# 64-bit weights decoded by one pass on ScalarE and two on VectorE, and the order of all engines' work set anew

## The chip, the cores and the metric

The kernel runs on one core of a Trainium2 chip. The metric is the device time of one execution in microseconds (us); the median of several runs counts. The core's engines work side by side, each through its own list of instructions in order: TensorE (PE in the profile, its weight loads PEld), VectorE (DVE), ScalarE (ACT), GpSimd (POOL) and SyncE (SP), which here only issues transfers. The 16 DMA engines carry those transfers.

## What is computed

Three layers, one after the other, on 2304 rows: attention with a window of 128 positions (8 heads of 64), a layer with a softmax-weighted activation and a layer norm (512 to 1024 to 512), and a gated layer (512 to 2048 to 512). Cut to what matters:

```python
scores = scale * np.matmul(q, k.transpose(0, 1, 3, 2))      # (4, 8, 576, 576), masked to a window of 128
attn = softmax(scores + bias)
x = np.matmul(attn, v).transpose(0, 2, 1, 3).reshape(2304, 512)
h = x @ w_in                                                # 512 x 1024
solu = h * softmax(h)
ln = (solu - mean) / sqrt(var + 1e-6) * g_ln
x = ln @ w_out                                              # 1024 x 512
h = x @ w2_in                                               # 512 x 2048
out = (h * sigmoid(h)) @ w2_out                             # 2048 x 512
```

The four weight matrices are float64: a weight lies in memory as 8 bytes, two 32-bit words, low and high. All else is float32.

## The kernel before, in words

The rows are cut into 18 blocks of 128 (index i), and two blocks make a chunk (index c, 0 to 8). For a block: the scores of four pairs of heads on TensorE (`a_qk`, L615), mask and maximum on VectorE (L640), the exponential on ScalarE (L645), a split of the result into a high and a low float16 part (`a_parts`), a transpose by DMA (L672) or on TensorE (`turned_parts`, L520 to L523), the product with v (L692), the division (L705), and the same split and transpose for the next product. Then `m1_in` (L734) multiplies with w_in, `layer_norm` follows (L748 to L776), and for a chunk `m1_out` (L826) multiplies with w_out, `m2_in` (L863) with w2_in in eight steps j, and `m2_out` (L890) with w2_out. Every product is made of three float16 products: high by high, high by low, low by high.

The weights stay in SBUF as such pairs, 48 slots of 128x512: w_in in slots 0 to 7, w_out in 8 to 15, w2_in in 16 to 31, w2_out in 32 to 47. `load_weight` brings two slots at a time into a buffer `stage` (two of these, loads at L436, 512 KB each). `decode` turns the 64-bit pattern into a float32 by integer operations in three passes over 128x1024 on VectorE: L414 shifts the high word by 3 into the PSUM tile `bits`, L416 puts the top two bits back, L418 adds the top bits of the low word and writes slot pair `W`. There are 24 decodes. Of each matrix the sum of squares is taken (L444 to L462: squares on ScalarE or GpSimd, a column sum on TensorE, a reduction on VectorE), `norm_scale` makes a power of two of it (the last row is L400; `sw2in` is that of w2_in), and only then does `split_weight` scale and split the slots: scaling at L490 (ScalarE) or L487 (GpSimd), the high part at L335 (ScalarE), the low part at L340 (GpSimd), or, where the letter of the slot in `E_W` is V, the two steps L480 (ScalarE) and L482 (VectorE). So no `m2_in` can start before all eight decodes of w2_in (decodes 9 to 16) and its scale are done, and no `m2_out` before those of w2_out (17 to 24). Each of `xT`, `lnT`, `y16`, `e1` and the PSUM tile `mm1` has one buffer, so ahead of the first `m2_in` only four blocks of `m1_in` and one chunk of `m1_out` can run.

The order of the instructions is made before the launch by a list scheduler in the kernel (`Sched.solve`). Every operation has a priority, set by its kind and block in `at`, and costs in ns for each engine that may take it; the scheduler fills the engines by priority and writes out each engine's list. Where an operation may run on two engines, letters in tables (`ENG`, `E_W`) or the scheduler's estimate choose. SyncE's list is such a list too: a transfer whose source or buffer isn't ready holds up all behind it.

## Time and profile before

| | |
|---|---|
| median of 3 runs | 751.68 us (748.95 to 751.75) |
| span of the profiled execution | 748.5 us, first to last instruction; the runs above are 0.45 to 3.25 us longer |
| busy: PE, PEld, DVE, ACT, POOL | 685.3, 458.8, 450.9, 400.5, 111.7 us |
| moved by DMA | 79.22 MB, mean 106 GB/s |

Busy time is the time in which an engine executes instructions; an average over the span mixes the stage in which weights arrive with the later one in which TensorE works without pause. PEclk in a stretch is the granted clock of TensorE as a share of full speed, 1.00 being 2.4 GHz and 0.50 being 1.2 GHz. The DMA share is the busy time of the core's 16 DMA engines in a stretch, over its length; in short stretches it can come out above 1.

### The profile page before, as it was taken

Reading aid. Unit: us, or ns where it says so; the run is one execution under the profiler, and the core shown is the slowest. Engines: PE = TensorE matmul, PEld = TensorE weight load, DVE = VectorE, ACT = ScalarE, POOL = GpSimd, SP = SyncE. Lnnn points to the kernel's source line nnn. Section 1 sums busy time; section 2 is a strip of 40 time slices with the busy share of each in tenths; the row PEclk is TensorE's granted clock in tenths of the full one; section 3 lists DMA queues with packets and bytes.
Section 4 is the critical chain, followed back from the end, with each engine's and each line's share of the span. In section 5 each row is a group of like instructions: output and inputs, shape, how many; then the busy total and the mean of one; then the engine's idle time right before and its main releaser. Section 6 shows DMA issues by size and latency. Waiting matters only on the chain.

```text
span 748.5 us, 13814 instructions
## 1 busy us (share of the span) xinstructions
PE 685.3 (92%) x5382; PEld 458.8 (61%) x5382; DVE 450.9 (60%) x1167; ACT 400.5 (54%) x850; POOL 111.7 (15%) x96
## 2 busy tenths in 40 slices
PE   2475777989999999999999999999999999999998
PEld 1233344776766558765666677757667767857853
DVE  3899899989868884887716655641552362222220
ACT  5597758998598864666714464431432352232231
POOL 2075321443276110100000100000100000000000
PEclk9996757899999999999999999999999999999999
DMA  9899996477864652847612235121210300200000
GB/s 244 281 301 235 221 258 207 140 156 173 167 122 107 146 125 51 151 105 152 154 29 43 62 81 85 29 57 23 42 36 15 57 29 4 54 29 1 2 28 29
DMA packets 139809, 79.22 MB, mean 106 GB/s; under 512 B 121696, under 2 KB 122336, under 8 KB 139744
## 3 DMA queue, kind: packets, MB, share of 16 engines
q1 hardware_dynamic: 139744, 78.34, 44.6%
q8 instruction: 42, 0.69, 0.4%
q14 instruction: 23, 0.19, 0.1%
HBM read 44.24 MB, written 4.72 MB: 65 GB/s over the span
## 4 chain that ended last, share of the span: by engine, by line
PE 80%; DVE 8%; DMA 5%; ACT 3%; issue 2%; POOL 1%; SPq 0%; DVEq 0%; ACTq 0%
PE mm L890 25%; PE mm L863 23%; PE mm L826 13%; PE mm L734 11%; PE sa L615 4%; PE sa L692 3%; DVE bits L416 1%; DVE W L418 1%; DVE e L640 1%; DMA stage<-in_moe_w_out_dram 1%; DVE bits L414 1%; DMA stage<-in_moe_w_in_dram 1%; DMA k<-in_kn_dram 1%; DMA lnT<-ln 1%; DMA aT<-a 1%
## 5 line engine op out<-in xcount | busy, mean ns | idle before, releaser
L863 PE MATMUL mm<-y,W 128*128 128x256 f16 x1728 | 210.4, 273 | 1.8 <-DVE t L873 1.8
L890 PE MATMUL mm<-W,g 128*128 128x512 f16 x864 | 207.5, 379 | 0.0
L863 PEld LDWEIGHTS <-W 128*128 128x128 f16 x1728 | 165.9, 98 | 39.3 <-issue 2.6
L890 PEld LDWEIGHTS <-g 128*128 128x128 f16 x864 | 82.5, 98 | 74.9 <-issue 0.2
L826 PE MATMUL mm<-lnT,W 128*128 128x256 f16 x864 | 110.0, 277 | 2.3 <-DVE aT L523 1.5
L734 PE MATMUL mm<-W,xT 128*128 128x512 f16 x432 | 103.2, 391 | 2.4 <-DVE W L482 0.9
L826 PEld LDWEIGHTS <-W 128*128 128x128 f16 x864 | 84.5, 99 | 22.8 <-DVE aT L523 1.8
L645 ACT ACTIVATE e<-e,mx 128x256 f32<-128x256 f32 (+1 forms) x144 | 70.1, 488 | 43.1 <-DVE mx L640 38.4
L876 DVE SCALAR_TENSOR_TENSOR g<-t,g 128x512 f16<-128x512 f32 x72 | 50.9, 708 | 59.9 <-ACT g L875 59.7
L875 ACT ACTIVATE g<-t 128x512 f16<-128x512 f32 x72 | 45.1, 627 | 75.8 <-PE mm L890 63.5
L872 ACT ACTIVATE t<-mm,cs 128x512 f32<-128x512 f32 x72 | 48.7, 679 | 60.1 <-PE mm L863 59.9
L873 DVE SCALAR_TENSOR_TENSOR t<-t,mm 128x512 f32<-128x512 f32 x72 | 48.9, 683 | 51.3 <-ACT t L872 50.9
L615 PE MATMUL sa<-k,q 64*128 64x128 f32 x544 | 58.4, 335 | 20.9 <-DVE mx L640 14.9
L734 PEld LDWEIGHTS <-xT 128*128 128x128 f16 x432 | 42.4, 100 | 52.8 <-issue 8.8
L615 PEld LDWEIGHTS sa<-k,q 64*128 64x128 f32 x544 | 42.7, 214 | 46.6 <-DVE mx L640 25.9
L640 DVE CUSTOM_DVE_ANT_0 e<-sa,table 128x256 f32<-128x256 f32 (+1 forms) x144 | 55.1, 401 | 26.5 <-PE sa L692 13.8
L692 PEld LDWEIGHTS <-aT 128*128 128x128 f16 x816 | 33.8, 102 | 20.7 <-DMA aT<-a 9.4
L692 PE MATMUL sa<-vs,aT 128*128 128x64 f16 x816 | 37.9, 200 | 8.5 <-DMA aT<-a 4.8
L335 ACT ACTIVATE a<-e 128x512 f16<-128x512 f32 (+1 forms) x68 | 40.3, 597 | 8.7 <-DMA aT<-a 7.8
L834 DVE SCALAR_TENSOR_TENSOR y<-mm,cs,y 128x512 f16<-128x512 f32 x18 | 13.5, 750 | 49.2 <-ACT y L831 49.2
L340 POOL TENSOR_TENSOR a<-e,a 128x512 f16<-128x512 f32 (+1 forms) x28 | 31.1, 1114 | 75.3 <-ACT a L335 74.7
L340 POOL TENSOR_TENSOR W<-W 128x512 f16<-128x512 f32 x31 | 37.7, 1230 | 25.8 <-ACT W L335 25.8
(133 smaller groups left out, 685.5 us busy)
## 6 DMA issues: line engine op xcount, KB each, us to landing
stage<-in_moe_w_in_dram SPq DMA_DIRECT2D x24, 512.0 KB, 6.0
stage<-in_moe_w_out_dram SPq DMA_DIRECT2D x24, 512.0 KB, 4.9
vraw<-in_vt_dram SPq DMA_DIRECT2D x34, 256.0 KB, 4.0
...
aT<-a SPq DMA_TRANSPOSE x68, 3.5
lnT<-ln SPq DMA_TRANSPOSE x34, 3.2
```

The costliest lines, as they stand in the source:

```text
L340: "G": ("G", cg(n), lambda: G.tensor_tensor(dst(), a(), b(), op), True)}
L615: T.matmul(SA[:, j, sl * P:(sl + 1) * P], q[rows, p, :], k[rows, p, :], start=True, stop=sl not in blank)
L640: v(n + 20, lambda j=j: V.tensor_tensor_reduce(e[:, j, lo:lo + n], SA[:, j, lo:lo + n], table[:, 2 * p + j, o:o + n], -0.125, 3.0e38, ALU. ...
L645: act(n, lambda j=j: A.activation(e[:, j, lo:lo + n], e[:, j, lo:lo + n], AF.Exp, bias=mx[:, j:j + 1], scale=-1.0, accum_out=rs[:, 2 * p + ...
L692: T.matmul(heads()[:, h // 4, h % 4, :], t[:, (2 * ha + j) * nh + c, :], vb[sl][:, h, hv, :], start=(n == 0), stop=(n == 3 * nh - 1))
L734: T.matmul(pt[:, half * 512:(half + 1) * 512], x[:, hx, k, :], W16(2 * k + half, hw), start=(k == 0 and hx + hw == 0), stop=(k == KD - 1 a ...
L826: T.matmul(pt[:, ct % 2], W16(8 + k, hw)[:, ct * P:(ct + 1) * P], l[:, hx * KF1 + k, :], start=(k == 0 and hw + hx == 0), stop=(k == KF1 - ...
L863: T.matmul(pt[:, mm], W16(16 + 4 * k + m // 4, hw)[:, (m % 4) * P:(m % 4 + 1) * P], y[:, hx, k, :], start=(k == 0 and hw + hx == 0), stop= ...
L872: act(512, lambda: A.activation(t.tile, flat(pt.tile), AF.Tanh, scale=cs[:, 0:1]), [pt, (cs, 0)], [t], extra=1)
L873: v(512, lambda: V.scalar_tensor_tensor(out=t.tile, in0=t.tile, scalar=1.0, in1=flat(pt.tile), op0=ALU.add, op1=ALU.mult), [t, pt], [t])
L876: v(512, lambda: V.scalar_tensor_tensor(out=flat(g[:, 1]), in0=t.tile, scalar=2.0 ** -16, in1=flat(g[:, 0]), op0=ALU.mult, op1=ALU.subtrac ...
L890: T.matmul(pt.tile, g[:, hg, mm, b * P:(b + 1) * P], W16(32 + m, hw), start=(m == 0 and hg + hw == 0), stop=(m == KF2 - 1 and hg == 1))
```

## The change

For 22 of the 24 decodes (`DECODE` has an A) the high word is shifted and its top bits set by one instruction on ScalarE: Prelu, which multiplies the positive and the negative values by different constants, read from `stage` with a step of two words and written to `bits`. VectorE multiplies the low word in place by 2^-29 and caps it at 7, and a second pass joins the two into `W`. Decodes 1 and 12 keep the three passes.

Three more things change. The scaling on GpSimd (`tensor_scalar`) has a second operand, a multiplication by 1.0. For scaling, high part, low part and squares a table `PICK` now names the engine of each instruction, VectorE among them also where it was not a choice before. And the priorities are set anew: each kind has a slope of its own over the blocks and 308 single offsets (`LATER`).

```diff
     def at(self, kind, i, p=0):
-        self.prio = PITCH * i + RANK[kind] + 0.01 * p
+        self.prio = RANK[kind] + SLOPE.get(kind, PITCH) * i + 0.01 * p + LATER.get((kind, i), 0.0)
...
+    def scaled(pick, n, dst, src, by, r, w, pool=False):
+
+        alts = [("A", ca(n, 1), lambda: A.activation(dst(), src(), AF.Identity, scale=by()), False),
+                ("V", cv(n, True), lambda: V.tensor_scalar(dst(), src(), by(), None, ALU.mult), True)]
+        if pool:
+            alts.append(("G", cg1(n), lambda: G.tensor_scalar(dst(), src(), by(), 1.0, ALU.mult, ALU.mult), True))
+        s.op(alts, r, w, pick=pick)
...
+        if DECODE[at // 2] == "A":
+            both = [(st, 0), (st, 1)]
+
+            act(1024, lambda: A.activation(flat(t.tile.bitcast(F32)), flat(st.tile.bitcast(F32)[:, :, :, 1]), AF.Prelu,
+                                           scale=2.0 ** 16, alpha=-2.0 ** 32), both, [t])
+            v(1024, lambda: V.tensor_scalar(flat(st[:, :, :, 0]), flat(st[:, :, :, 0]), 2.0 ** -29, 7.0, ALU.mult,
+                                            ALU.min), both, [(st, "low")], fast=True)
+            v(1050, lambda: V.scalar_tensor_tensor(out=out(), in0=t.tile, scalar=3, in1=st[:, :, :, 0],
+                                                   op0=ALU.logical_shift_left, op1=ALU.bitwise_or),
+              [(st, "low"), t], w)
+            return
...
-                if E_W[b] == "H":
-                    pool_(512, lambda: G.tensor_scalar(W[:, a, :], W[:, a, :], scl(), None, ALU.mult),
-                          [(W, a), src], [(W, a)])
-                else:
-                    act(512, lambda: A.activation(W[:, a, :], W[:, a, :], AF.Identity, scale=scl()),
-                        [(W, a), src], [(W, a)], extra=1)
-                copy("A", 512, lambda: W16(b, 0), lambda: W[:, a, :], [(W, a)], [(W, b)])
-                combine("G", 512, ALU.subtract, lambda: W16(b, 1), lambda: W[:, a, :], lambda: W16(b, 0),
+                scaled(("wc", b), 512, lambda: W[:, a, :], lambda: W[:, a, :], scl, [(W, a), src], [(W, a)], True)
+                copy(("wh", b), 512, lambda: W16(b, 0), lambda: W[:, a, :], [(W, a)], [(W, b)])
+                combine(("wl", b), 512, ALU.subtract, lambda: W16(b, 1), lambda: W[:, a, :], lambda: W16(b, 0),
                         [(W, a), (W, b)], [(W, b)])
...
+DECODE = "BAAAAAAAAAABAAAAAAAAAAAA"
...
-V_AT = [0, 1, 5, 9]
+V_AT = [0, 1, 5, 10]
```

What the new priorities make of the lists is seen in the lists themselves. In the new kernel L431 and L433 are the two VectorE passes of a decode, L429 is the Prelu, L341 and L352 are a high and a low part on VectorE, L346 is a scaling there, L412 the last row of `norm_scale`, L459 the weight load, and L690, L571 and L590 are the transfers that were L672, L553 and L572.

**VectorE, a decode of w2_in.** Before, rows around decode 14; `lnst` are the statistics of a layer norm, `xm` the attention's result:

```order
L748 TENSOR_REDUCE lnst<-mm_824 128x1
L414 TENSOR_SCALAR bits<-stage 128x1024
L749 TENSOR_SCALAR lnst<-lnst,sig_151 128x1
L416 SCALAR_TENSOR_TENSOR bits<-stage,bits 128x1024
L418 SCALAR_TENSOR_TENSOR W<-stage,bits 128x2x512
L752 TENSOR_SCALAR lnst<-lnst,sig_151 128x1
L705 TENSOR_TENSOR xm<-sa,rinv 128x512
```

The change, rows around decode 13:

```order
L431 TENSOR_SCALAR stage<-stage 128x1024
L767 TENSOR_SCALAR lnst<-lnst,sig_151 128x1
L486 TENSOR_REDUCE accw2in<-mm 128x1
L341 CAST a_909<-e 128x512
L433 SCALAR_TENSOR_TENSOR W<-bits,stage 128x2x512
L770 TENSOR_SCALAR lnst<-lnst,sig_151 128x1
L474 TENSOR_TENSOR sq<-W 128x512
L723 TENSOR_TENSOR xm<-sa,rinv 128x512
L772 RECIPROCAL lnst<-lnst 128x1
```

Three passes of a decode have become two, and passes that ScalarE or GpSimd had (a high part `a`, a square `sq`) stand between them.

**SyncE, the last loads of w2_in.** Before, with the loads of decodes 15 and 16 (`x4`) and then those of w2_out; `vraw` are rows of v, `aT` and `xT` transposes:

```order
L553 DMA vraw<-in_vt_dram 128x512
L672 DMA_TRANSPOSE aT<-a_959 128x8x128
L672 DMA_TRANSPOSE aT<-a_969 128x8x128
L436 DMA stage<-in_moe_w_in_dram 128x1024 x4
L553 DMA vraw<-in_vt_dram 128x512 x3
L553 DMA vraw<-in_vt_dram 128x256
L436 DMA stage<-in_moe_w_out_dram 128x1024 x2
L720 DMA_TRANSPOSE xT<-x_781 128x8x128
```

The change, with the loads of decode 16 (`x2`) and then those of decodes 17 to 19:

```order
L607 DMA k<-in_kn_dram 128x512
L608 DMA q<-in_qn_dram 128x512
L459 DMA stage<-in_moe_w_in_dram 128x1024 x2
L571 DMA vraw<-in_vt_dram 128x512
L690 DMA_TRANSPOSE aT<-a_1021 128x8x128
L459 DMA stage<-in_moe_w_out_dram 128x1024 x2
L690 DMA_TRANSPOSE aT<-a_1038 128x8x128
L459 DMA stage<-in_moe_w_out_dram 128x1024 x4
```

Ahead of the loads of decode 16 the new list has one load of v and two transposes `aT` less; behind them the loads of decodes 17 to 19 stand closer.

**VectorE, from the last sum of w2_in to its scale.** Before, the row `accw2in` is the last of the four sums, and the row of `sw2in` comes 14 rows behind this piece:

```order
L748 TENSOR_REDUCE lnst<-mm_1134 128x1
L462 TENSOR_REDUCE accw2in<-mm 128x1
L702 TENSOR_SCALAR rinv<-rsum 128x8
L749 TENSOR_SCALAR lnst<-lnst,sig_151 128x1
L703 RECIPROCAL rinv<-rinv 128x8
L392 TENSOR_REDUCE nrmb<-accw2in 128x1
L414 TENSOR_SCALAR bits<-stage 128x1024
L523 TENSOR_TENSOR lnT<-mm,lnT 128x4x128
L640 ISA e,mx<-sa,table 128x256
L640 ISA mx 128x1
```

The change, where the row of `sw2in` comes 9 rows behind the piece:

```order
L431 TENSOR_SCALAR stage<-stage 128x1024
L486 TENSOR_REDUCE accw2in<-mm 128x1
L433 SCALAR_TENSOR_TENSOR W<-bits,stage 128x1024
L723 TENSOR_TENSOR xm<-sa,rinv 128x512
L831 TENSOR_SCALAR shra<-mm 128x1
L404 TENSOR_REDUCE nrmb<-accw2in 128x1
L598 SCALAR_TENSOR_TENSOR vs<-vraw,sv_87,vs 128x8x64
L832 SCALAR_TENSOR_TENSOR shra<-mm,shra 128x1
L405 TENSOR_SCALAR nrmb<-nrmb 128x1
L770 TENSOR_SCALAR lnst<-lnst,sig_151 128x1
```

Before, of decode 17 only the first pass stands ahead of `sw2in`; now both of its passes do, so its loads are waited for as well.

## Rows read from the trace of the kernel before

**Rows 1.** Six stretches: busy us (and instructions) of each engine.

```profile
core 0: us, PE busy (x) PEld busy (x) DVE busy (x) ACT busy (x) POOL busy (x), PEclk, DMA share, GB/s
0.00:127.75 127.75, 75.78 (x519) 42.38 (x519) 107.89 (x259) 89.42 (x218) 40.93 (x45) 0.82 0.94 256
127.75:149.56 21.81, 20.32 (x140) 14.40 (x136) 20.25 (x50) 19.62 (x37) 11.39 (x10) 0.81 0.41 119
149.56:219.55 69.99, 64.90 (x665) 50.44 (x662) 58.38 (x152) 56.17 (x133) 29.35 (x23) 1.00 0.76 157
219.55:748.50 528.95, 524.34 (x4070) 351.61 (x4067) 264.40 (x711) 235.35 (x465) 30.07 (x20) 1.00 0.29 62
0.00:112.00 112.00, 63.53 (x416) 34.84 (x417) 93.33 (x211) 77.29 (x187) 40.93 (x45) 0.82 0.96 257
112.00:127.75 15.75, 12.25 (x104) 7.53 (x102) 14.56 (x51) 12.13 (x31) 0.00 (x0) 0.82 0.82 248
```

**Rows 2.** The three decode passes, by groups: busy us, mean ns | idle before.

```profile
L414 DVE TENSOR_SCALAR bits<-stage 128x1024 uint32<-128x1024 uint32 x24 | 29.3, 1220 | 4.0 <-DMA stage<-in_moe_w_in_dram 3.4 <-DMA stage<-in_moe_w_out_dram 0.6
L416 DVE SCALAR_TENSOR_TENSOR bits<-stage,bits 128x1024 uint32<-128x1024 uint32 x24 | 29.3, 1222 | 0.1
L418 DVE SCALAR_TENSOR_TENSOR W<-stage,bits 128x1024 uint32<-128x1024 uint32 x24 | 29.1, 1213 | 0.1
```

**Rows 3.** Waits of VectorE for weight loads: us, times, longest.

```profile
DVE bits L414 <- DMA stage<-in_moe_w_in_dram: 3.4, 3, 2.7
```

**Rows 4.** Issues of transfers, from the page; KB each, us to landing.

```profile
stage<-in_moe_w_in_dram SPq DMA_DIRECT2D x24, 512.0 KB, 6.0
```

**Rows 5.** Timeline of VectorE and SyncE; start us, us.

```profile
127.75 0.14 DVE L400 TENSOR_SCALAR sw2in<-nrmd 128x1 f32<-128x1 f32 x1
102.28 4.06 SPq L436 DMA_DIRECT2D stage<-in_moe_w_in_dram  x4
```

**Rows 6.** Timeline of TensorE, where its dense work begins; start us, us.

```profile
130.46 13.28 PE L826 MATMUL mm<-lnT,W 128*128 128x256 f16 x96 [1.49 <-DVE aT L523]
143.58 5.34 PE L734 MATMUL mm<-W,xT 128*128 128x512 f16 x24
149.56 1.48 PE L863 MATMUL mm<-y,W 128*128 128x256 f16 x12
219.55 2.75 PE L890 MATMUL mm<-W,g 128*128 128x512 f16 x12
```

**Rows 7.** Groups by shape that price the added passes: busy us, mean ns.

```profile
L774 DVE TENSOR_SCALAR e<-e,lnst 128x1024 f32<-128x1024 f32 x6 | 4.9, 811 | 0.1
L334 DVE CAST x<-xm 128x512 f16<-128x512 f32 x7 | 3.0, 424 | 6.5 <-DMA xT<-x 6.5
L339 DVE TENSOR_TENSOR a<-e,a 128x512 f16<-128x512 f32 x36 | 25.2, 702 | 8.6 <-ACT a L335 8.5
L640 DVE CUSTOM_DVE_ANT_0 e<-sa,table 128x256 f32<-128x256 f32 x128 | 51.0, 416 | 23.9 <-PE sa L692 12.8 <-PE sa L615 9.0 <-PE sa L621 0.8
L523 DVE TENSOR_TENSOR aT<-mm,aT 128x512 f16<-128x512 f32 x4 | 2.7, 683 | 0.2 <-ACT aT L522 0.2
L759 ACT ACTIVATE mm<-e,lnst 128x1024 f32<-128x1024 f32 x18 | 19.9, 1108 | 5.9 <-DVE lnst L758 5.9
L335 ACT ACTIVATE W<-W 128x512 f16<-128x512 f32 x31 | 18.8, 618 | 0.5 <-POOL W L340 0.5
L449 ACT ACTIVATE sq<-W 128x512 bf16<-128x512 f32 x22 | 12.8, 620 | 7.2 <-DVE W L418 4.1 <-DVE nrmb L389 2.9
L487 POOL TENSOR_SCALAR W<-W,sw2out 128x512 f32<-128x512 f32 x6 | 10.6, 1781 | 0.5 <-DVE sw2out L400 0.5
L340 POOL TENSOR_TENSOR W<-W 128x512 f16<-128x512 f32 x31 | 37.7, 1230 | 25.8 <-ACT W L335 25.8
```

**Rows 8.** Timelines of GpSimd and VectorE at one moment; start us, us.

```profile
53.04 1.16 POOL L340 TENSOR_TENSOR W<-W 128x512 f16<-128x512 f32 x1 [1.29 <-ACT W L335]
53.15 1.07 DVE L537 COPY sig<-sig 64x3 f32<-64x3 f32 x1
```

More of the change, by code (lines that the diff above doesn't have):

```diff
@@ L85, in before, with op @@
         return self.pred.get(o, ())
-    def op(self, alts, r=(), w=(), dma=0):
+    def op(self, alts, r=(), w=(), dma=0, pick=None):
+        if pick is not None:
+            name, j = pick
+            alts = [x for x in alts if x[0] == PICK[name][j]] or alts
         o = Op(alts, self.prio, len(self.ops), dma)
@@ L318, in cg, with cg1 @@
         return 215 + 1.98 * n
+    def cg1(n):
+        return 215 + 1.05 * n
     def v(n, fn, r=(), w=(), fast=False, port=False):
@@ L401, in norm_scale, with decode @@
         return big, scl
-    def decode(st, slots):
+    def decode(st, slots, at):
         t = Buf(ps_early, [P, 2, 512], U32, "bits", 1)
@@ L974 @@
 PITCH = 3.3
-RANK = {"table": -104.3, "vnorm": -66.9, "vload": 632.4, "vsplit": 82.3, "load": -243.6, "qk": -57.4,
-        "max": -161.5, "exp": 217.8, "parts": -218.7, "aturn": -111.4, "av": 179.9, "evac": -188.6,
-        "xturn": -57.5, "in": -119.2, "max1": 91.3, "norm": -233.0, "lparts": -421.0, "out": -334.0,
-        "share": -317.7, "y": -192.5, "in2": 186.3, "gate": -449.4, "out2": 257.1, "store": -337.1}
-WAT = {0: (65.8, 0.0, 85.1, 0.0), 8: (-155.1, 0.0, -336.6, 0.0), 16: (49.3, 0.0, 5.2, 0.0),
-       32: (144.1, 0.0, -16.4, 0.0)}
@@ L987, in WEIGHT @@
-def WEIGHT(slot0, at, split=False):
-    a, b, c, d = WAT[slot0]
-    return c + d * at if split else a + b * at
+RANK = {"aturn": 3681.5, "av": 497.5, "evac": -1913.9, "exp": 3035.5, "gate": -1087.6, "in": -116.5, "in2": 365.8,
+        "load": -2917.0, "lparts": -2005.2, "max": -131.3, "max1": 221.3, "norm": -5561.5, "out": -734.9,
+        "out2": 653.6, "parts": -1369.3, "qk": 489.8, "s0": 76.7, "s16": 404.9, "s32": -1212.4, "s8": 2638.4,
+        "share": -580.0, "store": 2676.3, "table": -3238.9, "vload": 7.5, "vnorm": 206.7, "vsplit": 377.6,
+        "w0": 1305.9, "w16": 17.6, "w32": 1146.2, "w8": 16.7, "xturn": -509.3, "y": 209.5}
@@ new lines @@
+SLOPE = {"aturn": 35.85, "av": -12.14, "evac": 25.91, "exp": 11.88, "gate": -14.56, "in": 18.98, "in2": -2.05,
+         "load": 13.07, "lparts": 3.11, "max": -4.74, "max1": 19.24, "norm": -7.64, "out": 20.97, "out2": 18.8,
+         "parts": -5.19, "qk": 19.89, "s0": 18.25, "s16": 6.74, "s32": 2.73, "s8": 8.69, "share": 12.97,
+         "store": 1.79, "table": 26.88, "vload": 9.62, "vnorm": 19.65, "vsplit": -0.07, "w0": -2.23, "w16": -5.62,
+         "w32": -0.22, "w8": -3.53, "xturn": 24.33, "y": -19.05}
```

96 lines of the change are left out of this document (69 added, 27 removed), and 25 rows, old and new, of the table LATER.

## The prediction

> **What bounds the kernel now.** I read the stretches first [rows 1]. From 219.55 us on TensorE is busy for 524.34 of 528.95 us at full clock; from 149.56 to 219.55 us it loses 5.1 of 69.99 us. The time that could be saved lies ahead of that: up to 127.75 us TensorE works 75.78 us, while VectorE is busy for 107.89 us (84%; 93.33 of the first 112 us, 83%, and 14.56 of the next 15.75). The page's other full resource is loading: up to 112 us the DMA share is 0.96 at 257 GB/s, 28.8 MB. So two things are nearly full at once, VectorE and the DMA engines, and that is the crux here.
>
> Next the timelines, for what ends this stretch. `sw2in`, the scale of w2_in, is ready at 127.75 us [rows 5]; the dense work of TensorE begins with `m1_out` of the first chunk (L826) at 130.46 us, goes on with `m1_in`, and the first `m2_in` (L863) stands at 149.56, the first `m2_out` (L890) at 219.55 us [rows 6]. Since no `m2_in` can run before all of w2_in is decoded and scaled, and the buffers allow only one chunk ahead of it, an earlier `sw2in` moves the whole rest. Thirdly the decodes: 24 times three passes of 1.22 us, 87.7 us of VectorE [rows 2]. It waited for loads of w_in and w2_in (one name in the rows) in only three places, 3.4 us together [rows 3], so it kept up with loading and no more.
>
> **The change, part by part.** All sums are against the profiled execution, 748.5 us; the runs shown are 0.45 to 3.25 us above it, so its span and the median differ by 3.2 us, and I add one or two.
>
> *VectorE up to the scale of w2_in.* Of the three passes the old list has 17, 16 and 16 ahead of `sw2in`: 49 x 1.22 = 59.7 us. The new one has two decodes of the old kind (6 passes, 7.3 us) and 15 of each new pass. The second new pass is like L418, 1.213 us: 18.2 us. The first, a multiplication with two operands from SBUF to SBUF, isn't in the trace; the nearest row is L774, of the same shape and form, at 811 ns, and the bound above is L414, which reads `stage` with the same step of two words at 1220 ns [rows 2, 7]. I take 0.81, since both its sides are in SBUF where L414 writes PSUM: 12.2 us (18.3 at the bound). Saved: 59.7 - 37.7 = 22.0 us (15.9).
>
> The new lists hand work to VectorE in return, ahead of the same row: 13 more casts and scalings of 512 columns at 424 ns (5.5 us), four more subtractions and five squares at about 0.7 (6.1 us, the lone small rest included) [rows 7]. Against that six mask passes (L640, 416 ns and a short reading behind each) and three turned parts (L523, 683 ns) now stand behind it, with some small ones: -5.8 us. Net: 22.0 - 11.6 + 5.8 = 16.2 us less (10.1 with the first pass at the bound). By VectorE alone `sw2in` would come at 127.75 - 16.2 = 111.5 us.
>
> *ScalarE and GpSimd.* A Prelu of 128x1024 isn't in the trace. The nearest row is L759, 1024 elements of float32 with PSUM on one side, 1108 ns; bounds are twice the 618 of a 512-column pass (1.24 us) and, if each sign took a pass of its own, 2.2 us [rows 7]. I take 1.1: 22 x 1.1 = 24 us. In exchange it loses some 52 us of high parts, scalings and squares over the whole span, so it gets freer by 28 us; at 2.2 it would still gain 4. The Prelu stands ahead of both VectorE passes' end and adds its 1.1 us once, to the last decode. The second operand on GpSimd costs nothing or saves some of 1781 ns per scaling; the engine worked 40.93 of the first 127.75 us, which covers it [rows 1].
>
> *Loading caps this.* Before, the loads of decodes 15 and 16 were issued from 102.28 us on, and with 6.0 us from issue to landing the last was there at about 112 us, VectorE waiting little [rows 4, 5]. The new SyncE list has one load of v and two transposes less ahead of decode 16 (about 0.8 MB): 28.0 MB, at 257 GB/s 109 us, where 111.5 us from VectorE would suit it. But both passes of decode 17 now stand ahead of `sw2in` on VectorE, which works in order: its 1 MB, a load of v and a transpose beside it, 1.6 MB, 6.1 us more, are to be in first: 115 us (111 if the share were 1.0). Then the Prelu 1.1, a pass 1.2 and the rows between it and `sw2in`, three of 0.7 us and a dozen small ones (4.1 us) follow: 121.5 us (117 at full share). I take 120. The gain here is 7.75 us instead of 16.2, because a wait for loads takes the place of half the passes removed.
>
> *From there to the first m2_in.* Before 2.7 us to L826 and 19.1 us from there to L863 [rows 5, 6]. In the new list `m1_out` stops after six products for a transpose of the next attention block, and a normalisation and a turned part stand between: I count 4.5 us, L826 at 124.5. The 19.1 us become 19.5 by eight more turned transposes. First `m2_in` at 144, 5.5 us earlier.
>
> *Behind it.* The 5.1 us that TensorE loses up to 219.55 us stand beside a ScalarE of 56.17 and a VectorE of 58.38 us in 70 [rows 1]. In the new lists either has about 7 us less there (fewer scalings on the one, six decodes of w2_out on the other). I count 3.5 of the 5.1 as regained. After the first `m2_out` only 4.6 us were lost, so nothing can be won there. Sum: 5.5 + 3.5 = 9, span 739.5, time 740.
>
> **A rule on the ports.** The row that speaks most against this change: on VectorE a copy of three elements took 1.07 us when it started 0.11 us after a GpSimd subtraction of 1.16 us, and ended with it [rows 8]. The casts, scalings and first passes added are of the kind that the same might happen to, 28 of them ahead of `sw2in`. The Trainium skill ("SBUF — State Buffer", Who interferes with whom) says why: GpSimd and VectorE share a pair of ports, an instruction that takes the double rate needs it alone, and whoever comes second waits for the whole of the first. The trace agrees in this place, 1.07 us. By the rule alone all such passes beside a busy GpSimd lose up to one GpSimd instruction each; by the row on how busy that is (40.93 of 127.75) about a third of them meet one, and half of its length is left: 28 x 0.32 x 0.6 = 5 us, which the wait for loads hides, as VectorE would have been 8.5 us early.
>
> **The rivals.**
> *Loading doesn't cap* (0.18). For it: VectorE also finished its passes late before, and a slower consumer holds back its own loads by the two `stage` buffers, so 257 GB/s may be what VectorE asked for. Against it: a share of 0.96. The Trainium skill ("Advanced Engine Details and Errata", DMA Bandwidth Details) gives 27.2 GB/s for each of 16 engines, so its estimate for 28.8 MB is 66 us; the trace doesn't agree, with 257 GB/s at 0.96. If this goes so, `sw2in` comes 16.2 us earlier and 4 to 5 lost us are regained: 748.5 - 20.5 = 728.
> *The gain is eaten* (0.14). The new lists wait in order for other things: `m1_out` behind the transposes, splits on VectorE behind decodes, TensorE's first `m2_out` behind the decodes of w2_out. It takes 9 us of new waits: 749, no measurable change. For it: the old lists lose just 4.6 us in the last 529, which any new order can only worsen.
> *Slower, by the ports* (0.10). If two-operand and cast passes of VectorE wait each time for GpSimd, it decides at 16.2 / 28 = 0.58 us a pass; at a whole subtraction of 1.16 us (or 1.23, its mean) each it is 32 us, `sw2in` 16 us later than before: 764. Half-way, 757. Against it: GpSimd is busy for a third of the stretch only.
> *Much faster* (0.06): both of the first two fall well and TensorE has no gap left: 722.
> *The decode doesn't become cheaper*: if the first pass runs at 1.22 us, 10.1 us are saved instead of 16.2, `sw2in` at 117.6 by VectorE, still under the 120 that loading allows: 740 to 742. This is inside the likeliest.
>
> **How the numbers follow.** The likeliest (0.52) has 740 as its middle and 734 to 746 for its own range: 3.5 us for the share of DMA, 3 us for the stalls. A measurement here can tell about 0.5% from no change, 747.9 to 755.4 us. Faster: 0.52 + 0.18 + 0.06 and a little of the third, 0.77. Same: 0.13; slower: 0.10. The range goes from the second case's 728, less one, to 753, which leaves out the slower case and the much faster one.
>
> **What would show it.** In the changed profile: the Prelu near 1.1 us, the first pass near 0.81 (1.22: the bound; over 1.2 with long ones between: the ports), the second at 1.21. `sw2in` (L412) at 120 us, with VectorE waiting for `stage` ahead of it some 8 us; 112 and no wait would be the second case, over 128 the fourth. DMA share up to 112 us near 0.96. The first `m2_in` near 144, the first `m2_out` near 205 to 212, TensorE's idle time behind it under 5 us. Wrong would be: `sw2in` early and the end not, so that a wait behind 150 us has given it back; or a decode whose stages wait for one another, since Prelu, first pass and second pass need the same `stage` and `bits`, and `bits` has one buffer.

## The result, and the profile after

The changed kernel takes 740.86 us (739.52 to 742.03, 4 runs) against 750.32 us (747.23 to 751.75, 4 runs): ratio 0.988, 95% interval 0.9848 to 0.9911. Its profiled execution spans 740.3 us, 8.2 less than the one of before. The forecast was 740 us. The time came out as forecast, but not by the road that was forecast: two terms of the sum were wrong and cancelled, which is luck.

First the stretch view of the kernel after. 117 us is where `sw2in` is ready, 140.17 us where the first `m2_in` begins; the piece from 62 to 82 us is explained below, and the last two rows are the 70 us behind the first `m2_in` and the rest.

```profile
core 0: us, PE busy (x) PEld busy (x) DVE busy (x) ACT busy (x) POOL busy (x), PEclk, DMA share, GB/s
0.00:117.00 117.00, 64.25 (x444) 35.39 (x445) 95.89 (x253) 85.81 (x187) 40.64 (x45) 0.85 0.95 264
62.00:82.00 20.00, 12.74 (x86) 7.21 (x86) 19.17 (x47) 13.86 (x30) 9.85 (x8) 0.50 0.97 226
0.00:140.17 140.17, 86.03 (x635) 51.98 (x635) 117.57 (x305) 106.22 (x233) 51.48 (x55) 0.85 0.89 245
140.17:740.30 600.13, 590.93 (x4752) 403.67 (x4748) 334.96 (x907) 271.69 (x566) 66.80 (x50) 1.00 0.34 75
140.17:210.17 70.00, 66.42 (x622) 50.14 (x619) 61.74 (x164) 51.50 (x113) 19.92 (x15) 1.00 0.59 147
210.17:740.30 530.13, 524.51 (x4133) 353.54 (x4130) 273.22 (x744) 220.20 (x454) 46.88 (x35) 1.00 0.31 65
```

The same view of the kernel before, where the first `m2_in` stood at 149.56 us:

```profile
62.00:82.00 20.00, 12.74 (x86) 7.25 (x84) 19.81 (x50) 18.90 (x43) 12.76 (x10) 0.52 1.05 259
0.00:149.56 149.56, 96.10 (x655) 56.77 (x655) 128.15 (x306) 109.04 (x254) 52.33 (x55) 0.82 0.87 236
149.56:748.50 598.94, 589.24 (x4732) 402.04 (x4728) 322.78 (x862) 291.51 (x597) 59.42 (x42) 1.00 0.35 73
```

The gain lies wholly ahead of the first `m2_in`: it begins 9.39 us earlier. From there to the end the kernel takes 600.13 us where it took 598.94, 1.2 more. TensorE's idle time there is 600.13 - 590.93 = 9.2 us, before 598.94 - 589.24 = 9.7; its work there grew by 1.7 us (4752 matmul records, 4732 before, at 5387 in all in both kernels: work of the first stage that the new list puts behind).

The groups of the new decode (columns as in [rows 2]):

```profile
L429 ACT ACTIVATE bits<-stage 128x1024 f32<-128x1024 f32 x22 | 24.3, 1104 | 6.6 <-DVE W L441 4.1 <-DVE lnst L786 1.4 <-DMA stage<-in_moe_w_out_dram 1.1
L431 DVE TENSOR_SCALAR stage<-stage 128x1024 uint32<-128x1024 uint32 x22 | 16.3, 743 | 0.7 <-DMA stage<-in_moe_w_in_dram 0.7
L433 DVE SCALAR_TENSOR_TENSOR W<-bits,stage 128x1024 uint32<-128x1024 uint32 x22 | 26.8, 1217 | 2.4 <-ACT bits L429 1.8 <-ACT vs L345 0.5
```

The Prelu takes 1104 ns, the first pass 743, the second 1217; the forecast had 1.1, 0.81 and 1.213 us. VectorE's wait for loads ahead of the 22 first passes is 0.7 us in all.

The timelines of VectorE and GpSimd in the kernel after, at the end of the first stage (start and length in us, and in brackets the idle time before and what ended it), and of TensorE behind it:

```profile
112.48 0.69 DVE L486 TENSOR_REDUCE accw2in<-mm 128x1 f32<-128x512 f32 x1 [1.36 <-PE mm L483]
116.89 0.14 DVE L412 TENSOR_SCALAR sw2in<-nrmd 128x1 f32<-128x1 f32 x1
109.14 2.87 POOL L473 TENSOR_TENSOR sq<-W 128x512 bf16<-128x512 f32 x2 [8.20 <-DVE mx L658]
```

```profile
120.76 1.46 PE L847 MATMUL mm<-lnT,W 128*128 128x256 f16 x6
122.67 9.39 PE L847 MATMUL mm<-lnT,W 128*128 128x256 f16 x84
140.17 5.42 PE L884 MATMUL mm<-y,W 128*128 128x256 f16 x48
```

`sw2in` is ready at 116.89 us, 10.86 earlier than in [rows 5]. The last wait ahead of it is not for a load: VectorE stands 1.36 us for a column sum, which waits for two squares that GpSimd makes from 109.14 us on. From `sw2in` to `m1_out` it takes 3.87 us, from there to the first `m2_in` 19.41 us.

### The profile page after: what moved, and what is told of

Same layout as the page of the kernel before. It is cut to its first block, busy times and chain, and to the rows that moved or that the text cites. A ratio compares the mean times of both kernels' runs of the same rounds, so it can differ in the third digit from the quotient of the medians.

```text
span 740.3 us, 13851 instructions
## 1 busy us (share of the span) xinstructions
PE 677.0 (91%) x5382; PEld 455.6 (62%) x5382; DVE 452.5 (61%) x1210; ACT 377.9 (51%) x797; POOL 118.3 (16%) x105
## 4 chain that ended last, share of the span: by engine, by line
PE 79%; DVE 9%; DMA 5%; ACT 4%; issue 2%; POOL 1%; SPq 0%; DVEq 0%; ACTq 0%; POOLq 0%
PE mm L911 24%; PE mm L884 24%; PE mm L752 12%; PE mm L847 11%; PE sa L633 5%; PE sa L710 3%; DMA stage<-in_moe_w_out_dram 2%; DVE e L658 1%; DVE W L433 1%; DMA xT<-x 1%; DMA aT<-a 1%; PE mm L483 1%; ACT e L663 1%; DVE xm L723 1%; DMA q<-in_qn_dram 1%
## 5 line engine op out<-in xcount | busy, mean ns | idle before, releaser
L847 PE MATMUL mm<-lnT,W 128*128 128x256 f16 x864 | 106.4, 274 | 0.0
L353 POOL TENSOR_TENSOR a<-e,a 128x512 f16<-128x512 f32 (+1 forms) x41 | 48.8, 1194 | 291.8 <-ACT a L340 213.1
L897 DVE SCALAR_TENSOR_TENSOR g<-t,g 128x512 f16<-128x512 f32 x72 | 53.6, 747 | 45.1 <-ACT g L896 44.8
L633 PE MATMUL sa<-k,q 64*128 64x128 f32 x544 | 56.6, 327 | 16.8 <-DVE mx L658 8.4
L633 PEld LDWEIGHTS sa<-k,q 64*128 64x128 f32 x544 | 41.1, 207 | 41.8 <-DVE mx L658 19.4
L766 DVE TENSOR_REDUCE lnst<-mm 128x1 f32<-128x1024 f32 x18 | 22.0, 1220 | 48.9 <-PE mm L752 48.9
L710 PEld LDWEIGHTS <-aT 128*128 128x128 f16 x816 | 33.9, 101 | 21.1 <-issue 10.1
L768 ACT ACTIVATE e<-mm,lnst,sig 128x1024 f32<-128x1024 f32 x18 | 21.6, 1200 | 46.4 <-DVE lnst L767 43.2
L353 POOL TENSOR_TENSOR ln<-e,ln 128x1024 f16<-128x1024 f32 x7 | 14.9, 2129 | 165.1 <-ACT ln L340 102.4
```

What stands on the lines that cost most here:

```text
L353: ("G", cg(n), lambda: G.tensor_tensor(dst(), a(), b(), op), True)], r, w, pick=pick)
L633: T.matmul(SA[:, j, sl * P:(sl + 1) * P], q[rows, p, :], k[rows, p, :], start=True, stop=sl not in blank)
L710: T.matmul(heads()[:, h // 4, h % 4, :], t[:, (2 * ha + j) * nh + c, :], vb[sl][:, h, hv, :], start=(n == 0), stop=(n == 3 * nh - 1))
L847: T.matmul(pt[:, ct % 2], W16(8 + k, hw)[:, ct * P:(ct + 1) * P], l[:, hx * KF1 + k, :], start=(k == 0 and hw + hx == 0), stop=(k == KF1 - ...
L897: v(512, lambda: V.scalar_tensor_tensor(out=flat(g[:, 1]), in0=t.tile, scalar=2.0 ** -16, in1=flat(g[:, 0]), op0=ALU.mult, op1=ALU.subtrac ...
```

## The experiments

The ratio of each row is against executions of the kernel before that were taken beside it, with medians of 748.95 to 750.32 us, so kernels of different rows are best compared by ratio. The places of `sw2in` and `m2_in` come from one profiled execution of each kernel, and the executions of one kernel differ by 1 to 4.5 us. "idle" is the length of the stretch from the first `m2_in` to the end, less TensorE's busy time in it. In all but the two with old priorities, whose lists are made anew, every row stands where it stood in the kernel named, and only what a row executes is changed or, with more loads, added to.

| kernel | median us | ratio to before (95%) | sw2in | first m2_in | from there to the end | idle in it |
|---|---|---|---|---|---|---|
| before | 750.32 | | 127.75 | 149.56 | 598.94 | 9.7 |
| after | 740.86 | 0.988 (0.9848 to 0.9911) | 116.89 | 140.17 | 600.13 | 9.2 |
| after, more loads | 744.72 | 0.9935 (0.9916 to 0.9955) | 121.03 | 144.61 | 598.89 | 8.0 |
| after, no first pass | 737.56 | 0.9848 (0.9822 to 0.9874) | 111.38 | 134.95 | 599.05 | 8.1 |
| after, three passes | 779.06 | 1.0397 (1.0373 to 1.0421) | 142.02 | 167.26 | 609.74 | 15.8 |
| before, new decode | 752.02 | 1.0037 (1.0022 to 1.0051) | 131.02 | 151.79 | 600.81 | 11.2 |
| before, new decode and engines | 764.94 | 1.0206 (1.0181 to 1.023) | 137.30 | 159.10 | 605.70 | 14.8 |
| old priorities, new decode | 757.79 | 1.0109 (1.0083 to 1.0134) | 122.93 | 148.06 | 608.64 | 12.6 |
| old priorities, new decode and engines | 757.04 | 1.0095 (1.0067 to 1.0123) | 126.52 | 152.07 | 605.93 | 11.5 |
| after, casts back on ScalarE | 748.60 | 0.999 (0.9974 to 1.0006) | 119.45 | 146.11 | 600.89 | 10.2 |
| after, two squares on ScalarE | 742.06 | 0.9897 (0.9875 to 0.9919) | 116.51 | 139.56 | 599.34 | 8.7 |
| after, one operand on GpSimd | 742.62 | 0.9907 (0.9889 to 0.9925) | 117.67 | 141.05 | 599.75 | 8.6 |
| after, all decodes new, two squares | 739.15 | 0.9851 (0.9834 to 0.9868) | 114.93 | 138.38 | 599.92 | 9.2 |

**What sets the pace of the first stage: loading or VectorE.** The forecast rested on loading. The first kernel adds loads to the kernel after:

```diff
+    jk = Buf(early, [P, 512, 2], U32, "junk", 1)
...
                     SP.dma_start(st[:, z].rearrange("p c e -> p (c e)"), view[:, k, f, :])
+                    if slot0 == 16 and z == 1:
+                        SP.dma_start(jk.tile.rearrange("p c e -> p (c e)"), view[:, k, f, :])
```

> The changed kernel with one more load of 512 KB beside each of the eight decodes of w2_in, into a buffer that nobody reads: 4.2 MB more ahead of sw2in. Theory L: at 268 GB/s 15.6 us more, sw2in near 132, time near 756. Theory V: the loads have room, sw2in moves by less than 4 us, time 741 to 745.

```profile
0.00:112.00 112.00, 62.00 (x396) 33.06 (x396) 87.76 (x229) 77.94 (x169) 35.87 (x41) 0.83 1.04 288
```

```profile
121.03 0.14 DVE L412 TENSOR_SCALAR sw2in<-nrmd 128x1 f32<-128x1 f32 x1
144.61 5.42 PE L889 MATMUL mm<-y,W 128*128 128x256 f16 x48
```

The longest new wait of VectorE in it, by the view of waits up to its `sw2in` (us, times, longest):

```profile
DVE a L341 <- DMA aT<-a: 3.4, 1, 3.4
```

4.2 MB more cost 4.1 us, not 15.6. In the first 112 us the DMA engines now move 288 GB/s at a share of 1.04, where they moved 268 at 0.97 in the changed kernel (the same view of it, to 112 us) and 257 at 0.96 before. So a share of 0.96 was not the end of what they carry: theory L falls, though theory V's bound of 4 us is just passed as well. VectorE waits for weight loads (`stage<-in_moe_w_in_dram`) no longer than before, 0.6 us against 0.7; the 3.4 us are one wait for a transpose of the attention, which reads the buffer `a` that VectorE is to write next. Loading is near, not binding.

The second takes VectorE work out of the kernel after:

```diff
-            v(1024, lambda: V.tensor_scalar(flat(st[:, :, :, 0]), flat(st[:, :, :, 0]), 2.0 ** -29, 7.0, ALU.mult,
-                                            ALU.min), both, [(st, "low")], fast=True)
-            v(1050, lambda: V.scalar_tensor_tensor(out=out(), in0=t.tile, scalar=3, in1=st[:, :, :, 0],
-                                                   op0=ALU.logical_shift_left, op1=ALU.bitwise_or),
+            v(1024, lambda: None, both, [(st, "low")], fast=True)
+            v(1050, lambda: V.tensor_scalar(out(), t.tile, 3, None, ALU.logical_shift_left), [(st, "low"), t], w)
```

> The changed kernel without the first VectorE pass of the new decode, and the second only shifts: the lowest three bits of 22 decodes' weights are left out. VectorE has 15 x 0.73 = 11.0 us less ahead of sw2in, all loads as before. Theory V: sw2in near 106 us, time near 730. Theory L: sw2in stays within 2 us of 116.9, time 739 to 741.

```profile
0.00:111.52 111.52, 63.85 (x444) 35.61 (x445) 87.02 (x238) 84.84 (x187) 40.51 (x45) 0.86 1.00 284
```

```profile
111.38 0.14 DVE L412 TENSOR_SCALAR sw2in<-nrmd 128x1 f32<-128x1 f32 x1
134.95 5.41 PE L881 MATMUL mm<-y,W 128*128 128x256 f16 x48
```

```profile
DVE W L432 <- ACT bits L429: 3.4, 5, 1.8
```

`sw2in` comes 5.5 us earlier, just half of the 11.0 us that the passes left out add up to, and loading goes along at 284 GB/s and a share of 1.00. VectorE's busy time falls by 8.9 us (95.89 to 87.02), less than the 11.0, since its instructions overlap a little at their ends. Of the 3.4 us between 8.9 and 5.5, most is the wait in the last line, again from the view of waits up to `sw2in`: its second passes now wait 3.4 us for the Prelu's result, where they waited 0.5 us in the kernel after. Neither theory has it whole: VectorE sets a part of the stage, and the rest is waits among the engines. How large a part is less sure than the trace makes it look. The median is only 3.3 us lower, though the first `m2_in` comes 5.2 us earlier (the two profiled executions took 735.79 and 742.03 us, further apart than the medians), and by ratio, 0.9848 (0.9822 to 0.9874) against 0.988 (0.9848 to 0.9911), the intervals overlap.

**Does one part of the change alone do it.** The new lists with the old decode:

```diff
+            def three():
+                V.tensor_scalar(flat(t.tile), flat(st[:, :, :, 1]), 3, 0x3FFFFFFF, ALU.logical_shift_left, ALU.bitwise_and)
...
-            act(1024, lambda: A.activation(flat(t.tile.bitcast(F32)), flat(st.tile.bitcast(F32)[:, :, :, 1]), AF.Prelu,
-                                           scale=2.0 ** 16, alpha=-2.0 ** 32), both, [t])
...
+            act(1024, lambda: None, both, [t])
+            v(1024, lambda: None, both, [(st, "low")], fast=True)
+            v(1050, three, [(st, "low"), t], w)
```

> The new lists as they are, but every decode takes the old three passes on VectorE, all three where the second new pass stood; nothing else moves, and ScalarE has no Prelu. Theory V (VectorE's list in order sets when sw2in is ready): each of 15 decodes ahead of sw2in costs 3 x 1.22 instead of 0.73 + 1.22 us, 1.71 us more, 25.6 us together: sw2in near 142 us instead of 116.9, the time near 764 us, 13 slower than before, so the rearranged lists alone lose. Theory L (loading sets it, VectorE has some 8 us to spare ahead of sw2in): sw2in near 134, time near 757.

```profile
0.00:142.16 142.16, 68.67 (x444) 39.25 (x445) 121.93 (x268) 70.74 (x171) 39.26 (x45) 0.79 0.78 218
```

`sw2in` comes at 142.02 us, theory V's 142, and VectorE is busy for 121.93 of the first 142.16 us. Here it does set the pace. The time is worse still than theory V's 764, since behind the first `m2_in`, where the last decodes of w2_out still stand in VectorE's list, another 9.6 us are lost (609.74 against 600.13). This takes the old passes in lists that were made for the new ones; lists made anew for the old decode with the new priorities and engines were not tried.

The old lists with the new decode:

```diff
+        def first():
+            A.activation(flat(t.tile.bitcast(F32)), flat(st.tile.bitcast(F32)[:, :, :, 1]), AF.Prelu,
+                         scale=2.0 ** 16, alpha=-2.0 ** 32)
+            V.tensor_scalar(flat(st[:, :, :, 0]), flat(st[:, :, :, 0]), 2.0 ** -29, 7.0, ALU.mult, ALU.min)
+        v(1050, first, [st], [t])
+        v(1050, lambda: None, [st, t], [t])
+        v(1050, lambda: V.scalar_tensor_tensor(out=out(), in0=t.tile, scalar=3, in1=st[:, :, :, 0],
+                                               op0=ALU.logical_shift_left, op1=ALU.bitwise_or), [st, t], w)
```

> The old lists as they are, but every decode is the new one: Prelu on ScalarE and the first VectorE pass where the first old pass stood, the second where the third stood, nothing where the second stood. Theory V: ahead of sw2in 17 first passes at 0.73 and 16 second ones at 1.22 instead of 59.7 us, 27.8 us less: sw2in near 100 us, time near 723 us, better than the changed kernel. Theory L: the 28.8 MB that are loaded ahead of decode 16 take 107 us at the 268 GB/s seen after the change, with 6 us of work behind: sw2in not before 113, time near 735.

The stretch view of it, to its `sw2in`, and from 62 to 82 us:

```profile
0.00:131.16 131.16, 74.21 (x520) 41.22 (x520) 83.94 (x244) 105.77 (x235) 42.83 (x45) 0.85 0.89 249
62.00:82.00 20.00, 9.42 (x78) 6.11 (x79) 15.60 (x40) 19.12 (x36) 10.88 (x9) 0.58 0.97 255
```

Both theories fall. VectorE is relieved of 24 us ahead of `sw2in` (83.94 busy, 107.89 in [rows 1]), loading runs at 0.89, and `sw2in` comes 3.3 us later. The second row shows one place where it goes: from 62 to 82 us ScalarE is busy for 19.12 of 20 us. It had been for 18.90 of 20 before, and in the kernel after it is for 13.86 (both in the result's views). VectorE, full there before with 19.81, is down to 15.60. In this piece the weights of w_out are scaled and split, squares are made, and now Prelus are added to that. In the chain of waits ScalarE's lines hold about 84% of this piece, where they held some 55% before.

That explains a delay, but not why `sw2in` gains nothing. The rows in front of it show more. First in the kernel before (SyncE, then TensorE), then here (SyncE, TensorE, VectorE):

```profile
117.94 0.78 SPq L589 DMA_DIRECT2D k<-in_kn_dram  x1
124.40 1.22 PE L615 MATMUL sa<-k,q 64*128 64x128 f32 x8 [0.57 <-DMA k<-in_kn_dram]
```

```profile
120.72 0.54 SPq L591 DMA_DIRECT2D k<-in_kn_dram  x1
127.67 1.23 PE L617 MATMUL sa<-k,q 64*128 64x128 f32 x8 [1.95 <-DMA k<-in_kn_dram]
129.04 0.42 DVE L642 CUSTOM_DVE_ANT_0 e<-sa,table 128x256 f32<-128x256 f32 x1 [2.22 <-PE sa L623]
```

In the old lists the mask passes of an attention block stand on VectorE ahead of `sw2in`. They need that block's scores, the scores need its rows of k, and SyncE issues the load of k at 117.94 us (before) or 120.72 us (here), behind a transpose `xT`. `sw2in` follows the issue by 9.81 and 10.30 us, and VectorE, freer now, stands still for 2.22 us for the scores. So in these lists a cheaper decode couldn't bring `sw2in` much ahead of this load, the sixth of k. In the kernel after, the sixth is issued at 120.76 us, 3.9 us behind `sw2in`, and the fifth at 95.10: the mask passes that need the sixth no longer stand in front of the scale. A run that moves these rows alone was not made.

So a theory of balance: the new decode pays if ScalarE is relieved at the same time. The old lists with the new decode and, of the new table, the engines for high parts and squares, for the splits of v and for most subtractions, each pass in its old place (two of the places in the code; the scalings, the parts of x and the low part of the layer norm keep their engines):

```diff
+                    def square():
+                        on = PICK["sq"][slot0 + at]
+                        if on == "A":
+                            A.activation(sq.tile, W[:, sl, :], AF.Square)
+                        else:
+                            (V if on == "V" else G).tensor_tensor(sq.tile, W[:, sl, :], W[:, sl, :], ALU.mult)
...
-        copy("A", 2 * n, lambda: part(0), src, [e], [(a, 0)])
+        copy("A", 2 * n, lambda: part(0), src, [e], [(a, 0)], PICK["ah"][4 * i + p])
```

> The old lists with the new decode, as in the run that gained nothing, and on top of it the engines that the new table names for high parts, squares, splits of v and subtractions, each in its old place. Theory B (balance: with the new decode alone ScalarE sets the pace, and the new table is what relieves it): ScalarE loses about 10 passes of 0.62 us ahead of sw2in, 6 us; sw2in near 124 or earlier, time 741 to 746. Theory O (the order does it: in the old lists the scores, loads and splits stand where they suited the old decode): time 749 to 754, sw2in 128 to 132.

```profile
0.00:137.44 137.44, 75.40 (x520) 42.52 (x520) 95.67 (x263) 96.46 (x215) 44.94 (x46) 0.82 0.85 238
```

764.94 us: the balance theory falls in this form, and it is worse than both forecasts. VectorE (95.67) and ScalarE (96.46) are now evenly loaded, and each stands still for 41 of 137 us. From 62 to 82 us ScalarE is busy for only 13.46 us here, so a full ScalarE alone is not what holds the old lists back. The load of k is issued at 127.60 us, and `sw2in` follows it by 9.70 us. With every engine's list in order, a pass that is handed to another engine stands there behind other rows than it did (which of them made this kernel 12.9 us slower than the run before it was not taken apart); evenly loaded engines alone gained nothing.

The rest of the change is the priorities. Two kernels in which the scheduler makes the lists anew: first the old priorities and engines with the new decode, then the changed kernel with the old priorities. (In both `RANK`, `PITCH` and `WAT` are those of before; the second keeps `DECODE`, `PICK`, `E_W` and `NORM` of the change.)

```diff
-        self.prio = RANK[kind] + SLOPE.get(kind, PITCH) * i + 0.01 * p + LATER.get((kind, i), 0.0)
+        if kind[0] in "ws" and kind[1:].isdigit():
+            self.prio = WEIGHT(int(kind[1:]), i, kind[0] == "s") + 0.01 * p
+        else:
+            self.prio = PITCH * i + RANK[kind] + 0.01 * p
```

> The old priorities and old engines with the new decode (22 of 24), but the lists are made anew by the scheduler for it, where the run with the old lists kept every row in its place. Theory S (the lists only have to be made for the passes that stand in them; the old priorities are good enough): ScalarE still has the 17 Prelus as an extra, but the waits of the frozen lists go: sw2in 118 to 122, time 740 to 744. Theory O (the new priorities and engines are needed): sw2in 126 to 132, time 747 to 754.

> The changed kernel, decode and table of engines and all, with the old priorities in place of slopes and single offsets; lists made anew. Theory S: within 4 us of the changed kernel, 738 to 745. Theory O: sw2in 122 to 130, time 746 to 754: then the offsets alone are worth what the change gains.

The stretch view of the first of the two, to its `sw2in` and behind its first `m2_in`, then of the second to its first `m2_in`:

```profile
0.00:123.08 123.08, 70.31 (x454) 38.37 (x455) 84.78 (x222) 98.61 (x217) 40.57 (x43) 0.81 0.92 255
148.06:188.00 39.94, 33.50 (x288) 25.97 (x287) 31.37 (x85) 35.01 (x78) 7.60 (x6) 0.91 0.66 172
148.06:756.70 608.64, 596.00 (x4770) 406.07 (x4768) 319.43 (x881) 298.40 (x608) 55.67 (x40) 0.99 0.34 73
```

```profile
0.00:152.07 152.07, 88.16 (x618) 51.64 (x618) 123.14 (x310) 107.42 (x236) 50.57 (x54) 0.84 0.87 236
```

757.79 and 757.04 us. Theory S falls in both by the time, and O's times are passed; of O's places for `sw2in` the second kernel's 126.52 us fits, while the first one's 122.93 us lies nearer to S. The first is instructive: its `sw2in` comes 4.8 us earlier than before and its first `m2_in` 1.5 us, yet it ends later by 8. From 148.06 to 188 us TensorE is idle for 6.4 of 39.94 us, and its clock is 0.91, not 1.00; behind the first `m2_in` its work takes 596.0 us instead of 589.2, with 38 more matmul records in it and part of them at the lower clock. What is won ahead is given back behind. The second differs from the kernel after by the priorities alone: its first `m2_in` comes 11.9 us later, and from there to the end it takes 5.8 us more. So the new priorities are worth some 16 us to the new decode and engines (757.04 against 740.86).

**What was handed to VectorE, and the ports.** Casts and scalings back on ScalarE, in the lists of the kernel after:

```diff
-              ("V", cv(n, True), lambda: V.tensor_copy(dst(), src()), True)], r, w, pick=pick)
+              ("V", cv(n, True), lambda: A.activation(dst(), src(), AF.Copy), True)], r, w, pick=pick)
...
-                ("V", cv(n, True), lambda: V.tensor_scalar(dst(), src(), by(), None, ALU.mult), True)]
+                ("V", cv(n, True), lambda: A.activation(dst(), src(), AF.Identity, scale=by()), True)]
```

> The changed kernel with every cast and one-operand scaling that VectorE was handed back on ScalarE, in its place. Ahead of sw2in VectorE loses 13 of them, measured at 8.7 us together, ScalarE gains 13 x 0.62 = 8 us. Theory B: ScalarE (85.8 of the first 117 us busy) becomes the slower of the two, sw2in 2 to 6 us later, time 743 to 747. Rival P (the ports: on VectorE those passes take 0.65 to 0.8 us instead of 0.42 since they wait for GpSimd, and delay the chain): sw2in 3 to 6 us earlier, time 735 to 738.

```profile
0.00:119.60 119.60, 63.86 (x444) 34.84 (x445) 89.66 (x240) 92.46 (x200) 39.27 (x45) 0.87 0.94 259
```

```profile
119.45 0.15 DVE L412 TENSOR_SCALAR sw2in<-nrmd 128x1 f32<-128x1 f32 x1
146.11 5.40 PE L884 MATMUL mm<-y,W 128*128 128x256 f16 x48 [0.17 <-DVE aT L541]
```

748.60 us: nearly all of the gain is gone. `sw2in` comes 2.6 us later, with ScalarE now the busier of the two (92.46 of 119.60), and the first `m2_in` 5.9 us later, as the splits of w2_in stand on ScalarE as well. Theory B holds here, though the time passes its 747 by a little, and rival P falls: in the new lists these passes belong on VectorE. But the ports do cost. In the kernel after, VectorE's groups ahead of `sw2in` (first view) and single passes beside GpSimd's (timelines):

```profile
L341 DVE CAST W<-W 128x512 f16<-128x512 f32 x4 | 2.8, 730 | 0.0
L341 DVE CAST a<-e 128x512 f16<-128x512 f32 x4 | 2.6, 657 | 0.0
L346 DVE TENSOR_SCALAR W<-W,swin 128x512 f32<-128x512 f32 x3 | 2.4, 833 | 0.0
```

```profile
44.75 1.17 DVE L431 TENSOR_SCALAR stage<-stage 128x1024 uint32<-128x1024 uint32 x1
100.12 1.38 DVE L352 TENSOR_TENSOR a<-e,a 128x512 f16<-128x512 f32 x1
42.92 2.45 POOL L353 TENSOR_TENSOR W<-W 128x512 f16<-128x512 f32 x2
99.79 1.15 POOL L353 TENSOR_TENSOR a<-e,a 128x512 f16<-128x512 f32 x1 [8.45 <-ACT a L340]
```

The casts take 730 and 657 ns where [rows 7] have 424. The first pass at 44.75 us takes 1.17 instead of about 0.68 us and ends 0.55 us behind GpSimd's subtraction; the subtraction at 100.12 us, which reads two tiles, takes 1.38 instead of 0.70 and ends 0.56 us behind GpSimd's. The Trainium skill ("SBUF — State Buffer", Who interferes with whom) says that of a VectorE instruction in a two-port mode (the double rate) and a GpSimd instruction the one that starts first keeps the shared ports to its end and the other waits, and that a VectorE instruction with two inputs from SBUF contends with a GpSimd instruction that reads SBUF; these rows agree. Over the stage the excess of casts, scalings, first passes and that subtraction is 1.2 + 0.9 + 1.1 + 0.8 + 0.7 = 4.7 us (scalings against the 480 ns of an undisturbed one, the 15 first passes at 733 ns against 680). Of the 15 first passes only two took over 0.70 us, 1.17 and 0.93, and both began well before a GpSimd instruction ended.

The wait for the two squares on GpSimd:

```diff
-                          ("G", cg(512), lambda: G.tensor_tensor(sq.tile, W[:, sl, :], W[:, sl, :], ALU.mult), True),
+                          ("G", cg(512), lambda: A.activation(sq.tile, W[:, sl, :], AF.Square)
+                           if slot0 + at in (30, 31) else
+                           G.tensor_tensor(sq.tile, W[:, sl, :], W[:, sl, :], ALU.mult), True),
```

> The changed kernel with the last two squares of w2_in on ScalarE instead of GpSimd, in their place. In the profile of the changed kernel they took 2.88 us in a row on GpSimd and VectorE waited 1.36 us for the column sum behind them. If this wait is what sets sw2in: 1 to 2 us earlier, time 739 to 740. If VectorE's own work sets it: no change that can be told.

```profile
111.62 0.69 DVE L488 TENSOR_REDUCE accw2in<-mm 128x1 f32<-128x512 f32 x1 [1.10 <-PE mm L485]
116.51 0.14 DVE L412 TENSOR_SCALAR sw2in<-nrmd 128x1 f32<-128x1 f32 x1
```

The sum comes 0.86 us earlier, `sw2in` 0.38, and the medians don't tell the two kernels apart, so this wait was not what set `sw2in`. And the second operand of GpSimd's scaling:

```diff
-            alts.append(("G", cg1(n), lambda: G.tensor_scalar(dst(), src(), by(), 1.0, ALU.mult, ALU.mult), True))
+            alts.append(("G", cg1(n), lambda: G.tensor_scalar(dst(), src(), by(), None, ALU.mult), True))
```

> The changed kernel with GpSimd's scaling back at one operand. Ten such scalings took 691 to 956 ns with two operands and 1560 to 1781 ns with one before. GpSimd is busy for 40.6 of the first 117 us: if that cover holds, no change that can be told (within 1 us); if splits of w2_in behind sw2in wait for it, first m2_in 1 to 2 us later, time 742 to 743.

The group of w2_in's scalings on GpSimd in the kernel after, then in this one:

```profile
L348 POOL TENSOR_SCALAR W<-W,sw2in 128x512 f32<-128x512 f32 x3 | 2.0, 691 | 0.0
```

```profile
L348 POOL TENSOR_SCALAR W<-W,sw2in 128x512 f32<-128x512 f32 x3 | 5.2, 1745 | 0.0
```

A scaling takes 691 ns with two operands and 1745 with one, but ten of them move the first `m2_in` by 0.9 us, and the time by less than the measurement tells: 0.9907 (0.9889 to 0.9925) against 0.988 (0.9848 to 0.9911). So no gain of the second operand is shown in the time.

**A version from what was learnt.** VectorE's relief had moved `sw2in` by half its size in the trace, so decodes 1 and 12 get the new passes as well, in the manner of `first` above, and the two squares stay on ScalarE:

```diff
-        v(1050, lambda: V.tensor_scalar(flat(t.tile), flat(st[:, :, :, 1]), 3, 0x3FFFFFFF, ALU.logical_shift_left,
-                                        ALU.bitwise_and), [st], [t])
...
+        v(1050, first, [st], [t])
+        v(1050, lambda: None, [st, t], [t])
```

> The changed kernel with decodes 1 and 12 by the new passes too, Prelu and first pass where the first old pass stood, and the last two squares of w2_in on ScalarE. VectorE has 2 x 1.7 = 3.4 us less ahead of sw2in, ScalarE 2.2 us and two squares of 0.62 more. From the run without the first pass (11.0 us less for VectorE moved sw2in by 5.5) I expect half of 3.4 us, 1.7, less what ScalarE gives back: first m2_in 138 to 140, time 738 to 741. If ScalarE sets the two places (at the start it makes the mask table, in the middle it splits w_out): no gain, 741 to 743.

```profile
114.93 0.14 DVE L412 TENSOR_SCALAR sw2in<-nrmd 128x1 f32<-128x1 f32 x1
138.38 5.42 PE L888 MATMUL mm<-y,W 128*128 128x256 f16 x48
```

739.15 us (737.52 to 740.08), ratio 0.9851 (0.9834 to 0.9868): better than the kernel before, and the fastest of those that do the whole decode. Its first `m2_in` comes 1.8 us earlier than in the kernel after, as expected; the intervals of the two overlap, so it isn't shown to beat that one.

## Why the prediction was right, and where it was not

- **What bounds the kernel.** That the stage ahead of the first `m2_in` decides, and the rest follows at TensorE's pace, was right: in the kernel after and the six that keep its lists and the Prelu, 598.9 to 600.9 us follow behind the first `m2_in`, whatever happened ahead. That VectorE bounds that stage was right in part (11.0 us less gave 5.5 in the trace, and 3.3 in the median). That loading is full was wrong. And one thing it didn't see: in the old lists the rows in front of `sw2in` hang on a load of k, issued at 117.94 us; in the new lists this load and the rows that need it stand behind `sw2in`. In the kernel before the two were nearly level (VectorE waits 0.77 us for those scores); with the new decode in the old lists VectorE waited 2.22 us for them right ahead of `sw2in`.
- **The sum for VectorE** was good. Forecast: 16.2 us less up to `sw2in`. Measured: 107.89 to 95.89 us, 12.0 less; without the 4.7 us that the ports cost, it would be 16.7. The price of the Prelu was right, that of the first pass 0.07 us too high.
- **"Loading caps this"** is the step that failed. It held `sw2in` back to 120 us and spoke of some 8 us of waiting for `stage`; measured are 116.89 and 0.7 us, and 4.2 MB on top cost 4.1 us. The loads of decode 17, which it saw in at 115 us, were in when its first pass ran at 110.19. By VectorE's account the 5.3 us by which `sw2in` falls short of the 16.2 are the ports' 4.7 us, which the prediction worked out as 5 us and then let loading hide, and 1.2 us of longer waits (its idle time goes from 19.9 to 21.1 us), less the half microsecond by which its work fell more than the sum had it. What `sw2in` would do without the ports was not tried. This term gave 5.5 us at the first `m2_in` and measured 9.4.
- **From `sw2in` to the first `m2_in`** was right: 4.5 and 19.5 us forecast, 3.87 and 19.41 measured.
- **"I count 3.5 of the 5.1 as regained"** failed too. In the 70 us behind the first `m2_in` TensorE loses 3.6 us where it lost 5.1 [rows 1], so 1.5 came back; from there to the end it loses 5.6 us where it lost 4.6, and its work behind the first `m2_in` rose by 1.7. The piece grew by 1.2 us. The premise held for one engine only: either was to have about 7 us less there, and in these 70 us ScalarE has 4.7 less (51.50), but VectorE 3.4 more (61.74). All three waits of TensorE that its view of waits names in these 70 us (1.5, 1.2 and 0.9 us) are for VectorE. The first `m2_out` came at 200.93 us, ahead of the 205 to 212 that were expected, and that gained nothing at the end.
- The two errors, 3.9 us too little ahead and 4.7 too much behind, cancel to 0.8, and so 740 came out.
- **ScalarE** was summed up over the whole span: 24 us of Prelu against some 52 us handed away, 28 us freer. Its busy time fell from 400.5 to 377.9 us, 22.6 less. Where in time the Prelus fall was not asked: from 62 to 82 us ScalarE had no room before, and the new decode in the old lists lost time in that piece.
- **The rivals.** "Loading doesn't cap" had its premise right and its time, 728, wrong, since neither all 16.2 us nor the stalls came. The ports, the rival for slower, cost what was forecast and far less than the 16.2 us from which they decide.

No part that was tried alone gains; all of them together do. The new lists without the decode lose 4.0%, the decode in the old lists 0.4%, the decode in lists made anew with the old priorities 1.1%, decode and engines without the priorities about 1%, and decode and lists without the casts and scalings on VectorE come out at 0.999. New priorities and engines with the old decode, in lists made anew, were not tried. Which of the 308 offsets matter stays open. The change also sets anew which engine ends each layer norm (`NORM`) and which weight slots are split without a scaling of their own (`E_W`); every kernel made from the kernel after has these, and no run takes them apart.
